# In an attention and MLP kernel, the second weight is split in place, and the planner of the instruction order counts DMA semaphores

## Chip, core and metric

The kernel runs on one core of a Trainium2 chip. The metric is device time in microseconds (us) of one execution. The engines are named as in the profile: PE (TensorE, matmul) with PEld (its weight loads), DVE (VectorE), ACT (ScalarE), POOL (GpSimd) and SP (SyncE, which issues most transfers; ACT issues some too). "SPq" and "ACTq" are the instruction queues of SP and ACT.

## What is computed

Block-sparse attention over 4 batches, 8 heads, 768 positions and head size 64, followed by an MLP of 3072 tokens, 512 to 2048 to 512:

```python
mask = np.abs(blk_i - blk_j) <= window
mask = mask | (blk_i == 0) | (blk_j == 0) | (blk_i == n_blocks - 1) | (blk_j == n_blocks - 1)
for qb in range(n_blocks):
    for kb in sampled_blocks[qb]:
        mask[qb * block:(qb + 1) * block, kb * block:(kb + 1) * block] = True
scores = np.where(mask, scale * np.matmul(q, k.transpose(0, 1, 3, 2)), -1000000000.0)
...
attn = attn / (np.sum(attn, axis=-1, keepdims=True) + 1e-09)
x = np.matmul(attn, v)
...
h = x @ w_in
sp = np.where(h > 20.0, h, np.log1p(np.exp(np.minimum(h, 20.0))))
g = h * np.tanh(sp)
return (g @ w_out).astype(np.float32)
```

Blocks have 32 positions, so there are 24 of them; three sampled blocks belong to each block of queries.

## The kernel before

**Numbers in two halves.** Each large product is made of three float16 products: an operand a is scaled and split into hi (its float16) and lo (the float16 of what is left), and hi x hi, hi x lo and lo x hi are summed in PSUM. The two weights arrive as 64-bit numbers. VectorE decodes them into float32 with three integer instructions per piece (lines 873, 876 and 879). The scale of a weight comes from matmuls of it with itself (`gram`, line 361), a diagonal and a root (`add_gram`, `add_root`, `root`).

**First weight, w_in.** Eight pieces (`piece_i`, `load_i`) are loaded by ACT or SP into a ring of three buffers "wr", decoded and split by TensorE and casts (lines 947 to 956). `scales_w` (line 1016) writes `gsc` when all pieces have their scale.

**Second weight, w_out.** Sixteen chunks of 128x512 (`load_o`, `piece_o`) are loaded into buffers of the ring "raw", which has six and is shared with the loads of q, k and v, and decoded. The float32 of chunk fc takes the whole place `wo[:, fc]`, 2 KiB per partition, in which its hi and lo shall stand. So the split (`parts_o`, which calls `add_split` with `by_pe` false) first writes a scaled copy `wt` into another "raw" buffer (line 963 on ACT or 965 on DVE), casts it to hi (968 or 969), and lets POOL subtract for lo (970).

**Attention.** 52 jobs (13 per batch): a job takes two blocks of queries, or one dense one. It goes through scores (661), maximum (703 to 708), exponential (727), transposes (667), the split of the probabilities (750, 754; in the first three jobs through TensorE, 758 and 763), the product with v (789), division (808 to 811), a transpose and the split of x (836, 839). Its keys are gathered by POOL or ACT (595, 598), its values by SP's transfers from a copy of v in DRAM, "vd" (615 to 622).

**MLP.** Twelve tiles of 256 tokens. `moe_h` (1049) makes the hidden layer of a tile, which takes the x of jobs 0 to 4 for the first one; `moe_g` (1060 to 1099) the activation on ACT, DVE and POOL; `moe_y` (1114) the product with w_out of the tile before, between the pieces of the next tile's hidden layer. The hidden layer's products keep their order, and so do those with w_out. The product of the first half of the first tile with w_out takes all sixteen chunks.

**What sets the order.** `Plan.emit` is a list scheduler: it keeps an estimate of when each engine is free and when each task is ready, and issues, one by one, the task that would start first. Each task has a duration, engines that may run it, the ring buffers that it takes, and a key. The key comes from the call and from three tables, URGE (by kind of tensor), JOBS (by job, the first 14) and PIECES (by piece of a weight). It decides between tasks that could start within 0.02 us of each other; a smaller one goes first. `pace` ranks work on TensorE: the scores of job i are ranked as if they could not start before START[i], but go at once if TensorE has nothing else ready; jobs keep their order. A transfer's end is estimated from its queue alone, by its duration. `fill` puts matmuls without use (line 1309) in front of TensorE's work where it would idle between 14 and 200 us of the plan. On the chip each engine runs its instructions in this order and waits on semaphores. What a task waits for is named by r, what it writes by w.

Of the kernel before, what the change touches and what calls it, by code (L numbers as in the profile page):

```python
# [32 lines left out]
URGE = {"am": -30, "dgi": -29, "endsv": 24, "gh": 8, "gp": -3, "gram": 4, "gramv": 1, "hik": -7, "hiq": 20, "hiv": -7, "hs": 4, "hsw": -16, "k": -4, "kg": -1, "kw": -30, "mx": 19, "nb": -12, "o": 13, "p": -1, "ph": 2, "pl": -30, "q": 12, "r": 30, "rawk": 6, "rawq": 23, "rawv": 24, "s": -10, "sck": 12, "scq": -24, "scv": -3, "ssk": -22, "ssq": 1, "ssv": 9, "t": 14, "tpq": -30, "tpv": 2, "tpw": -12, "tx": -30, "us": -2, "v": -1, "vd": -9, "vg": 1, "wdi": -4, "whi": -3, "who": -30, "wli": -27, "wlo": -11, "wo": 19, "wor": 24, "wq": 7, "wr": -23, "ws": 1, "wto": 26, "xhw": 22, "xw": 10, "ys": -7}  # L33
JOBS = [-17, -8, 5, -19, 0, 1, -8, -9, -24, -11, 1, 1, -4, -26]
PIECES = [-4, -2, -1, 2, -1, 3, 5, 18, -23, -12, -10, -4, -3, -4, 3, 8, 7, 11, 13, 14, 16, 23, 31, 26]
# [29 lines left out]
class Plan:  # L65
# [4 lines left out]
    SEM = 0.06  # L70
# [53 lines left out]
    def emit(self, pace, fill):  # L124
# [6 lines left out]
        free, ready, dma, held = {}, {}, {}, {}  # L131

# [9 lines left out]
        while todo:  # L142
# [66 lines left out]
def attn_mish_kernel(ctx: ExitStack, tc: tile.TileContext, qT, kT, v, sampled, blocks, w_in, w_out, out):  # L209
# [11 lines left out]
    nc = tc.nc  # L221
# [106 lines left out]
    BOTH = True  # L328
# [70 lines left out]
    def add_root(key, ss, fn, r, after, w, new, cls, n=1, apart=False, ring="t"):  # L399

        add("PE", 0.3 * n, lambda: root_pe(key, ss(), apart, ring), r=r, w=[key], new=[(ring, key)], key=cls - 2, lat=0.3)
        add("DVE", 0.6, fn, r=[key, *after], w=w, new=new, key=cls)

    def load(b, what, js, ring="raw", after=()):
# [3 lines left out]
        def fn():  # L408
# [15 lines left out]
            kind=("dma", 1.95 * n))  # L424
# [130 lines left out]
    def globals_v(b, n):  # L555
# [3 lines left out]
        add("SP", 0.9, fn, r=VD3(b), w=[("vg", n)], key=-1, lat=2.3, kind=("dma", 0.5))  # L559
# [46 lines left out]
    def gather_v(su):  # L606
# [6 lines left out]
        def fn():  # L613
# [10 lines left out]
            kind=("dma", 0.9))  # L624

    def fetch_dense(su):
# [11 lines left out]
        for j in T3:  # L638
# [3 lines left out]
                key=-3, lat=2.4, kind=("dma", 2.0))  # L642
# [245 lines left out]
    def load_i(k):  # L888
# [5 lines left out]
        if wide:  # L894
            go = lambda eng: load_w(pools["w"], raw, "wr", src, None, eng)
            add("ACT", 0.45, lambda: go(nc.scalar), r=after, w=[raw], new=[("wr", raw)], key=-9, lat=2.0,
                kind=("dma", 3.9), also=[("SP", 0.5, lambda: go(nc.sync), False)] if BOTH else ())
            return
        add("ACT", 0.45, lambda: load_w(None, None, None, src, a0_i(k).rearrange("p (c f) -> p c f", c=NCC),
                                          nc.scalar), r=after,  # L900
            w=[key], key=-9, lat=2.0, kind=("dma", 1.95))
# [77 lines left out]

    def a0_o(fc):  # L980
        return wo[:, fc].rearrange("p t d -> p (t d)").bitcast(F32)

    def load_o(fc, after=()):
# [3 lines left out]
            key=-5, lat=2.0, kind=("dma", 1.95), also=[("SP", 0.5, lambda: go(nc.sync), False)] if BOTH else ())  # L987
# [47 lines left out]
    def moe_h(st, fp, part):  # L1035
# [17 lines left out]
        for f2 in range(2):  # L1053
            mlp(1.31 if part is None else 0.85, lambda f2=f2: fn(f2), r=[*PARTS_I(fp), *xs], w=[kh, "h in order"],
# [47 lines left out]
    def moe_y(st, m, k, last):  # L1102
# [4 lines left out]
        def fn(h2):  # L1107
# [3 lines left out]
            for f in range(2 * h2, 2 * h2 + 2):  # L1111
                fc = 4 * k + f
                for n, (g, w) in enumerate(((0, 0), (0, 1), (1, 0))):
                    nc.tensor.matmul(tl[ky], tl["g", b, t, k][:, g, f, q], wo[:, fc, w],  # L1114
# [5 lines left out]
        if k == NFC // 4 - 1:  # L1120
# [14 lines left out]
            add("SP", 0.4, out_fn, r=[kys], lat=2.0, kind=("dma", 1.1))  # L1135
# [222 lines left out]
```

## Time and profile before

| What | Value |
|---|---|
| time, median of 3 runs | 788.75 us (786.95 to 789.26) |
| span of the profiled execution, first to last instruction | 786.6 us |
| median less that span | 2.15 us |
| mean granted clock of TensorE | 0.990 |
| HBM read, written | 80.38 MB, 12.95 MB |

The span belongs to one profiled execution, for which no time of its own outside the span is given; the three times are of other executions. So sums made from the profile are made against the span, and the 2.15 us stand between it and the median. In the profile's rows an instruction's line is that of the kernel, "out<-in" are tensors with their buffer numbers left out, and "x16" is a count. A row of waits reads: engine and instruction, what it waited for, us in total, times, the longest.

### The profile page before, as it was taken

The numbers are of one execution on the slowest core, as the hardware profiler recorded it, in microseconds if no ns is written. First come the engines' busy times: TensorE is split into PE (matmuls) and PEld (weight loads), VectorE is DVE, ScalarE is ACT, GpSimd is POOL, SyncE is SP. The second block draws the span as 40 slices with busy tenths as digits, with TensorE's granted clock in tenths as the row PEclk, the third lists the DMA queues.
The fourth block names the chain that finished last, engine by engine and source line by source line (L and its number), as shares of the span: only waits on it lengthen the run. The fifth ranks groups of instructions, "written<-read, shape, count | busy, mean of one in ns | idle before, by whom it ended". The sixth has DMA issues, their size and how long they took to land.

```text
span 786.6 us, 30628 instructions
## 1 busy us (share of the span) xinstructions
PE 740.5 (94%) x12793; PEld 518.7 (66%) x12793; DVE 493.5 (63%) x900; ACT 542.7 (69%) x880; POOL 307.6 (39%) x393
## 2 busy tenths in 40 slices
PE   6677899888999999999999999999999999999997
PEld 5544578665577767767776676677677667666663
DVE  6868988998767764795866457656665453223220
ACT  3555778768868877777887768786876666455650
POOL 2114244887635542374443422534641331213021
PEclk9989999999999999999999999999999999999999
DMA  9878857104534475244346603523444112000000
GB/s 339 263 236 256 268 176 202 44 2 136 159 117 131 119 198 171 69 162 120 87 139 194 192 15 101 174 77 91 119 115 119 37 39 81 14 15 14 14 14 27
DMA packets 57742, 95.31 MB, mean 121 GB/s; under 512 B 8323, under 2 KB 20612, under 8 KB 57604
## 3 DMA queue, kind: packets, MB, share of 16 engines
q1 hardware_dynamic: 52032, 80.51, 34.9%
q10 hardware_dynamic: 5572, 12.85, 4.8%
q8 instruction: 100, 1.64, 0.9%
q14 instruction: 38, 0.31, 0.1%
HBM read 80.38 MB, written 12.95 MB: 119 GB/s over the span
## 4 chain that ended last, share of the span: by engine, by line
PE 73%; DVE 10%; ACT 6%; DMA 5%; issue 2%; POOL 1%; SPq 1%; POOLq 1%; ACTq 0%; DVEq 0%
PE h_None L1049 27%; PE y L1114 26%; PE obank L789 6%; PE t L667 6%; PE s L661 4%; DMA vg<-vd 3%; PE tx L667 1%; PE wd_i L947 1%; DVE wt_o L965 1%; DMA wr<-in_moe_w_in_dram 1%; DVE hs_None L1087 1%; DVE v L491 1%; DMA raw_k<-in_k_dram 1%; ACT us_None L1078 1%; POOL kt L522 1%
## 5 line engine op out<-in xcount | busy, mean ns | idle before, releaser
L1049 PE MATMUL h_None<-xh,wi 128*128 128x256 f16 x1536 | 282.8, 273 | 0.0
L1114 PE MATMUL y<-wo,g 128*128 128x512 f16 x1152 | 278.0, 380 | 4.0 <-POOL wo L970 2.6
L1049 PEld LDWEIGHTS <-wi 128*128 128x128 f16 x2304 | 223.5, 98 | 47.3 <-issue 2.1
L1049 PE MATMUL h_None<-xl,wi 128*128 128x256 f16 x768 | 209.8, 273 | 0.0
L1114 PEld LDWEIGHTS <-g 128*128 128x128 f16 x1152 | 111.1, 98 | 106.7 <-issue 7.3
L1099 POOL TENSOR_TENSOR g<-hs_None,g 128x1024 f16<-128x1024 f32 x48 | 107.6, 2241 | 188.4 <-DVE g L1096 144.8
L598 POOL COPY kg<-kt 128x256 f16 x258 | 107.2, 451 | 123.3 <-PE s L661 109.7
L1060 ACT ACTIVATE hs_None<-h_None,gsc 128x512 f32<-128x512 f32 x96 | 65.5, 684 | 80.2 <-PE h_None L1049 79.4
L727 ACT ACTIVATE pt<-s,nb,ns 128x256 f32<-128x256 f32 (+1 forms) x208 | 106.3, 582 | 5.7 <-PE t L667 5.0
L750 ACT ACTIVATE ph<-t 128x512 f16<-128x512 f32 x112 | 66.5, 596 | 45.1 <-PE t L667 45.0
L754 DVE SCALAR_TENSOR_TENSOR pl<-t,ph 128x512 f16<-128x512 f32 x105 | 71.9, 686 | 35.8 <-ACT ph L750 35.5
L1087 DVE SCALAR_TENSOR_TENSOR hs_None<-us_None,hs_None 128x1024 f32<-128x1024 f32 x48 | 65.0, 1355 | 40.1 <-ACT us_None L1086 40.1
L667 PE MATMUL t<-ident,pt 128*128 128x128 f32 x448 | 70.4, 280 | 6.8 <-DVE pl L754 3.6
L708 DVE TENSOR_REDUCE mx<-s 128x4 f32<-128x1024 f32 x44 | 53.7, 1222 | 31.9 <-PE s L661 31.3
L1083 POOL TENSOR_TENSOR us_None<-us_None 128x1024 f32<-128x1024 f32 x22 | 44.2, 2007 | 71.8 <-DVE us_None L1081 68.7
L667 PEld LDWEIGHTS t<-ident,pt 128*128 128x128 f32 x448 | 51.6, 142 | 21.4 <-DVE pl L754 4.5
L789 PEld LDWEIGHTS <-ph 128*32 128x32 f16 x3584 | 47.9, 94 | 20.9 <-issue 13.1
L1078 ACT ACTIVATE us_None<-hs_None,hsc 128x1024 f32<-128x1024 f32 x48 | 55.2, 1150 | 0.9
L789 PE MATMUL obank<-vg,ph 128*32 128x65 f16 (+1 forms) x3200 | 50.6, 196 | 4.0 <-DMA vg<-vd 2.2
L1081 DVE TENSOR_SCALAR us_None<-us_None 128x1024 f32<-128x1024 f32 x48 | 37.4, 778 | 25.4 <-ACT us_None L1078 25.2
L1085 ACT ACTIVATE us_None<-us_None 128x1024 f32<-128x1024 f32 x48 | 50.7, 1056 | 1.6 <-POOL us_None L1083 0.8
L1086 ACT ACTIVATE us_None<-us_None 128x1024 f32<-128x1024 f32 x48 | 50.7, 1056 | 0.8
(199 smaller groups left out, 893.6 us busy)
## 6 DMA issues: line engine op xcount, KB each, us to landing
vg<-vd SPq DMA_DIRECT2D x320, 65.0 KB, 2.6
vg<-vd SPq DMA_DIRECT2D x80, 195.0 KB, 3.2
wr<-in_moe_w_in_dram ACTq DMA_DIRECT2D x8, 1024.0 KB, 7.4
vd<-v SPq DMA_DIRECT2D x12, 520.0 KB, 3.8
vg<-vd SPq DMA_DIRECT2D x12, 520.0 KB, 5.1
raw_k<-in_k_dram SPq DMA_DIRECT2D x12, 512.0 KB, 5.4
raw_q<-in_q_dram SPq DMA_DIRECT2D x12, 512.0 KB, 4.3
raw_v<-in_v_dram SPq DMA_DIRECT2D x12, 512.0 KB, 5.0
```

The lines of the kernel that those rows point to most:

```text
L598: nc.gpsimd.tensor_copy(out=dst, in_=tl["kt", b][:, :, ds(j, BS)])
L667: nc.tensor.matmul(out, src, ident, start=start, stop=stop, is_transpose=True)
L727: ex = lambda o, x, g, w: nc.scalar.activation(out=o, in_=x, func=AF.Exp, bias=nb[:, g, w:w + 1], scale=tl["ns", b, sus[w]["qb"] // TB][:, ...
L750: nc.scalar.activation(out=new(sb, "ph", ("ph", i, j), [P, 2, 2, P], F16), in_=tl["t", i, j], func=AF.Copy, scale=PSC)
L754: nc.vector.scalar_tensor_tensor(out=new(sb, "pl", ("pl", i, j), [P, 2, 2, P], F16), in0=tl["t", i, j], scalar=PSC, in1=tl["ph", i, j], op ...
L789: nc.tensor.matmul(o[cs, w, g, 0:v1 - v0], p[:, k, g, cs], vt[:, k, 2 * c + g, v0:v1], start=j == 0 and g == 0 and k == 0 and n == 0, stop ...
L1049: nc.tensor.matmul(h[:, f2, 0:n].rearrange("p (s q) -> p s q", q=BS), wi[:, fp, cc // 2, w, cc % 2, fs], x[:, s0:s0 + sn, cc], start=f2 == ...
L1060: nc.scalar.activation(out=tl[kq][:, 2 * (fp % 2):2 * (fp % 2) + 2, 0:n], in_=tl[kh][:, :, 0:n], func=AF.Copy, scale=gsc[:, fp:fp + 1])
L1078: nc.scalar.activation(out=us(), in_=hs(), func=AF.Exp, scale=hsc[:, b:b + 1])
L1087: add("DVE", 1.32 * c, lambda: nc.vector.scalar_tensor_tensor(out=hs(), in0=us(), scalar=-0.5, in1=hs(), op0=ALU.add, op1=ALU.mult), r=[ku ...
L1099: add("POOL", 2.3 * c, lambda: nc.gpsimd.tensor_tensor(out=g(1), in0=hs(), in1=g(0), op=ALU.subtract), r=[kq, ("gh",) + kp], w=[kp], use=[kg])
L1114: nc.tensor.matmul(tl[ky], tl["g", b, t, k][:, g, f, q], wo[:, fc, w], start=fc == 0 and n == 0, stop=fc == NFC - 1 and n == 2)
```

## The change

There are four parts.

1. The second weight is split without the copy and without POOL. Chunk fc is cast from its float32 to hi with the scale in the same instruction (ACT or DVE), and DVE makes lo as float32 x scale - hi with one scalar_tensor_tensor. The halves go to `wo_at(fc)`, the place of the chunk two before, whose float32 is used up by then; the first two go to new room "wx" in the pool of the MLP (4 KiB per partition). So a cast waits for hi and lo of the chunk two before, or, for chunks 0 and 1, for the pool to be open.
2. In `add_root` the matmul waits for what the VectorE half waited for (`after`), and `moe_h` waits for `gsc`.
3. The planner counts eight semaphores ("lanes") for the transfers that SP and ACT issue and eight for POOL's. Transfers take them in turn, whatever their queue, and one starts only when the transfer eight before it has landed. A task names how many transfers it has, and some durations are new.
4. URGE, JOBS, PIECES and START have new values. In URGE most of the 50-odd entries change, by up to some 50 (the two long lines are left out below).

```diff
-JOBS = [-17, -8, 5, -19, 0, 1, -8, -9, -24, -11, 1, 1, -4, -26]
-PIECES = [-4, -2, -1, 2, -1, 3, 5, 18, -23, -12, -10, -4, -3, -4, 3, 8, 7, 11, 13, 14, 16, 23, 31, 26]
+JOBS = [-18, -3, 5, -18, -5, 14, -9, -16, -30, 8, -7, -18, -29, -7]
+PIECES = [-5, -4, -1, -1, 4, 25, 0, 20, -29, -29, 7, -5, -8, -11, 18, 7, 9, -2, 12, 15, 19, 27, 24, 14]
...
-    SEM = 0.06
+    SEM, LANES = 0.06, 8
...
+        lanes = {w: [[0.0] * self.LANES, 0] for w in ("hard", "soft")}
...
+                    if t.kind and t.kind[0] == "dma":
+                        lane, n = lanes["soft" if eng == "POOL" else "hard"]
+                        at = max(at, lane[n % self.LANES])
                     start = self.port(held, eng, max(at, f), t.ways[eng][2])
...
-                other = max([x for e, x in dma.items() if e != t.eng], default=0.0)
-                at = max(dma.get(t.eng, 0.0), end)
-                dma[t.eng] = at + t.kind[1] + min(t.kind[1], 0.5 * max(other - at, 0.0))
-                t.end = max(dma[t.eng], end + t.lat)
+                lane, n, end, t.end = *lanes["soft" if t.eng == "POOL" else "hard"], start, 0.0
+                each = t.kind[1] / t.kind[2]
+                for k in range(n, n + t.kind[2]):
+                    end = max(end, lane[k % self.LANES]) + t.dur / t.kind[2]
+                    other = max([x for e, x in dma.items() if e != t.eng], default=0.0)
+                    at = max(dma.get(t.eng, 0.0), end + 0.3)
+                    dma[t.eng] = at + each + min(each, 0.5 * max(other - at, 0.0))
+                    lane[k % self.LANES] = land = max(dma[t.eng] + 0.5, end + t.lat + min(max(other - end, 0.0), 3.5))
+                    t.end = max(t.end, land)
+                lanes["soft" if t.eng == "POOL" else "hard"][1] += t.kind[2]
+                free[t.eng] = end
...
-        add("PE", 0.3 * n, lambda: root_pe(key, ss(), apart, ring), r=r, w=[key], new=[(ring, key)], key=cls - 2, lat=0.3)
+        add("PE", 0.3 * n, lambda: root_pe(key, ss(), apart, ring), r=[*r, *after], w=[key], new=[(ring, key)], key=cls - 2, lat=0.3)
...
-            kind=("dma", 1.95 * n))
+            kind=("dma", 1.45 * n, n))
...
-            kind=("dma", 0.9))
+            kind=("dma", 1.5, 2 + NR - 1 + (w0 - qb != -1 or w1 - qb != 2)))
...
+    SH = 2
+
+    def wo_at(fc):
+
+        return pools["wx"][:, fc] if fc < SH else wo[:, fc - SH]
...
     def parts_o(fc, cls):
-        if fc == 0:
-            add_diag(("o",), lambda: sc_o, "sc_o", cls)
-        add_split(("o", fc), ("o",), lambda: a0_o(fc), wo[:, fc, 0], wo[:, fc, 1], ("wo", fc), RINGO, cls,
-                  lambda: sc_o, "sc_o", fc % 4 < OPE)
+
+        before = [(w, "o", fc - SH) for w in ("wh", "wl")] if fc >= SH else ["open"]
+        kh, kl = ("wh", "o", fc), ("wl", "o", fc)
+
+        def hi(eng):
+            if eng == "ACT":
+                nc.scalar.activation(out=wo_at(fc)[:, 0], in_=a0_o(fc), func=AF.Copy, scale=sc_o)
+            else:
+                nc.vector.tensor_scalar(out=wo_at(fc)[:, 0], in0=a0_o(fc), scalar1=sc_o, scalar2=None, op0=ALU.mult)
+        add("ACT", 0.62, lambda: hi("ACT"), r=[("wo", fc), "sc_o", *before], w=[kh], key=cls,
+            also=[("DVE", 0.45, lambda: hi("DVE"), True)])
+        add("DVE", 0.72, lambda: nc.vector.scalar_tensor_tensor(
+            out=wo_at(fc)[:, 1], in0=a0_o(fc), scalar=sc_o, in1=wo_at(fc)[:, 0], op0=ALU.mult, op1=ALU.subtract),
+            port=True, r=[("wo", fc), "sc_o", kh], w=[kl], key=cls)
...
-            mlp(1.31 if part is None else 0.85, lambda f2=f2: fn(f2), r=[*PARTS_I(fp), *xs], w=[kh, "h in order"],
+            mlp(1.31 if part is None else 0.85, lambda f2=f2: fn(f2), r=[*PARTS_I(fp), "gsc", *xs], w=[kh, "h in order"],
...
-                    nc.tensor.matmul(tl[ky], tl["g", b, t, k][:, g, f, q], wo[:, fc, w],
+                    nc.tensor.matmul(tl[ky], tl["g", b, t, k][:, g, f, q], wo_at(fc)[:, w],
...
+        pools["wx"] = pools["m"].tile([P, SH, 2, DM], F16, name="wx", tag="wx", bufs=1)
...
-        new=[("hs", ("z",))], key=-9, lat=6.0)
+        new=[("hs", ("z",))], key=-9, lat=6.0, kind=("dma", 0.9, 2 + B))
...
-    RES, START = 595.0, [0, 58, 39, 56, 33, 120, 63, 62, 76, 58, 107, 143, 72, 148]
+    RES, START = 595.0, [4, 107, 38, 81, 33, 149, 115, 59, 5, 106, 122, 170, 16, 77]
```

The other lines give the remaining transfers their count and remove switches that had one value.

More of the change, by code (lines that the diff above doesn't have):

```diff
@@ L28 @@
              wq=2, am=2, dg=2)
-URGE = {"am": -30, "dgi": -29, "endsv": 24, "gh": 8, "gp": -3, "gram": 4, "gramv": 1, "hik": -7, "hiq": 20, "hiv": -7, "hs": 4, "hsw": -16, "k": -4, "kg": -1, "kw": -30, "mx": 19, "nb": -12, "o": 13, "p": -1, "ph": 2, "pl": -30, "q": 12, "r": 30, "rawk": 6, "rawq": 23, "rawv": 24, "s": -10, "sck": 12, "scq": -24, "scv": -3, "ssk": -22, "ssq": 1, "ssv": 9, "t": 14, "tpq": -30, "tpv": 2, "tpw": -12, "tx": -30, "us": -2, "v": -1, "vd": -9, "vg": 1, "wdi": -4, "whi": -3, "who": -30, "wli": -27, "wlo": -11, "wo": 19, "wor": 24, "wq": 7, "wr": -23, "ws": 1, "wto": 26, "xhw": 22, "xw": 10, "ys": -7}
-JOBS = [-17, -8, 5, -19, 0, 1, -8, -9, -24, -11, 1, 1, -4, -26]
-PIECES = [-4, -2, -1, 2, -1, 3, 5, 18, -23, -12, -10, -4, -3, -4, 3, 8, 7, 11, 13, 14, 16, 23, 31, 26]
+URGE = {"am": -10, "dgi": -16, "endsv": 24, "gh": -20, "gp": -30, "gram": 17, "gramk": -27, "gramq": 30, "gramv": 13, "hik": -30, "hiq": 22, "hiv": 24, "hs": -13, "hsw": -18, "k": 25, "kg": 9, "kw": -24, "mx": 16, "nb": -18, "o": -2, "p": 1, "ph": 8, "pl": -17, "q": -7, "r": 23, "rawk": -30, "rawq": 17, "rawv": 22, "s": 4, "sck": 25, "scq": -28, "scv": 14, "ssk": -30, "ssq": -13, "ssv": -16, "t": -3, "tpk": -30, "tpq": 5, "tpv": -15, "tx": -15, "us": -11, "v": 18, "vd": -6, "vg": 26, "wdi": -4, "whi": -10, "who": -11, "wi": -4, "wli": -30, "wlo": -15, "wo": 18, "wor": 24, "wq": 5, "wr": -12, "ws": -30, "wto": 26, "xw": 7, "ys": -30}
+JOBS = [-18, -3, 5, -18, -5, 14, -9, -16, -30, 8, -7, -18, -29, -7]
+PIECES = [-5, -4, -1, -1, 4, 25, 0, 20, -29, -29, 7, -5, -8, -11, 18, 7, 9, -2, 12, 15, 19, 27, 24, 14]
 def place(w):
@@ L541, in store_v @@
             out=vd[b][j * TT:(j + 1) * TT].rearrange("(c p) h d -> p c h d", p=P), in_=tl["v", b, j]),
-            r=[("v", b, j)], w=[("vd", b, j)], key=-4, lat=2.5, kind=("dma", 2.0))
+            r=[("v", b, j)], w=[("vd", b, j)], key=-4, lat=2.5, kind=("dma", 2.0, 1))
     KT3 = lambda b: [("k", b, j) for j in T3]
@@ L558, in fn @@
                 nc.sync.dma_start(out=vgs[n][s * BS:(s + 1) * BS, 1], in_=vd[b][j * BS:(j + 1) * BS])
-        add("SP", 0.9, fn, r=VD3(b), w=[("vg", n)], key=-1, lat=2.3, kind=("dma", 0.5))
+        add("SP", 0.9, fn, r=VD3(b), w=[("vg", n)], key=-1, lat=2.3, kind=("dma", 0.5, 2))
     regs = {}
@@ L641, in fetch_dense @@
                 w=[("vg", j) if j < NVG else ("vt", b)], new=[("raw", ("vt", b))] if j >= NVG else (),
-                key=-3, lat=2.4, kind=("dma", 2.0))
+                key=-3, lat=2.4, kind=("dma", 2.0, 1))
     PROD = ((0, 0), (1, 0), (0, 1))
@@ L896, in load_i @@
             add("ACT", 0.45, lambda: go(nc.scalar), r=after, w=[raw], new=[("wr", raw)], key=-9, lat=2.0,
-                kind=("dma", 3.9), also=[("SP", 0.5, lambda: go(nc.sync), False)] if BOTH else ())
+                kind=("dma", 3.9, 1), also=[("SP", 0.5, lambda: go(nc.sync), False)])
             return
         add("ACT", 0.45, lambda: load_w(None, None, None, src, a0_i(k).rearrange("p (c f) -> p c f", c=NCC),
-                                          nc.scalar), r=after,
-            w=[key], key=-9, lat=2.0, kind=("dma", 1.95))
+                                        nc.scalar), r=after,
+            w=[key], key=-9, lat=2.0, kind=("dma", 1.95, 1))
     def piece_i(k, cls):
@@ L986, in load_o @@
         add("ACT", 0.45, lambda: go(nc.scalar), r=after, w=[raw] + ([] if wide else [("wo", fc)]), new=[("raw", raw)],
-            key=-5, lat=2.0, kind=("dma", 1.95), also=[("SP", 0.5, lambda: go(nc.sync), False)] if BOTH else ())
+            key=-5, lat=2.0, kind=("dma", 1.95, 1), also=[("SP", 0.5, lambda: go(nc.sync), False)])
     def piece_o(fc, cls):
@@ L1134, in moe_y @@
                 also=[("ACT", 0.7, lambda: ys_fn("ACT"), False)])
-            add("SP", 0.4, out_fn, r=[kys], lat=2.0, kind=("dma", 1.1))
+            add("SP", 0.4, out_fn, r=[kys], lat=2.0, kind=("dma", 1.1, 1))
     DL = 10
```

3 lines of the change are left out of this document (removed).

## The prediction, made before the changed kernel ran

> **What bounds the kernel now.** I read first the page's busy times and its forty slices, then the stretches between the kernel's stages.
>
> ```profile
> PE 740.5 (94%) x12793; PEld 518.7 (66%) x12793; DVE 493.5 (63%) x900; ACT 542.7 (69%) x880; POOL 307.6 (39%) x393
> PE   6677899888999999999999999999999999999997
> ```
>
> TensorE is busy for 94% of the span, and its low digits stand almost all at the front. The view of stretches (length, then busy time and instructions of each engine, granted clock, DMA share, GB/s) is cut at the first matmul of the hidden layer, at the start and the end of the second weight's split, and at 220 and 700 us:
>
> ```profile
> 0.00:102.60 102.60, 76.87 (x1619) 52.63 (x1619) 80.35 (x181) 59.10 (x116) 25.99 (x54) 0.95 0.84 272
> 102.60:138.00 35.40, 34.16 (x930) 29.49 (x923) 29.23 (x60) 29.31 (x54) 16.87 (x24) 1.00 0.65 183
> 138.00:185.00 47.00, 39.24 (x454) 28.05 (x452) 45.73 (x60) 35.41 (x51) 36.88 (x29) 0.96 0.12 38
> 185.00:220.00 35.00, 33.50 (x634) 19.71 (x633) 27.70 (x45) 26.29 (x43) 24.00 (x27) 1.00 0.45 137
> 220.00:700.00 480.00, 474.93 (x8657) 338.75 (x8656) 291.82 (x537) 352.58 (x577) 186.23 (x253) 1.00 0.39 110
> 700.00:786.60 86.60, 81.79 (x515) 50.09 (x513) 18.70 (x22) 39.98 (x43) 17.66 (x8) 0.99 0.05 19
> L1309 PE MATMUL obank<-neg 128*128 128x240 f16 x109 | 15.6, 282 | 3.8 <-DVE xs L811 3.8
> ```
>
> TensorE's idle time is length less busy: 25.7, 1.2, 7.8, 1.5, 5.1 and 4.8 us, 46.1 in all. The last row is the filler of line 1309, 15.6 us of work without use. So 61 us of the span are not useful TensorE work. From 220 us on there is little to win: 5.1 us in 480, and a tail whose end is the last output. What can move lies before 185 us, in two places.
>
> The first is 138 to 185 us: there VectorE is busy 45.7 of 47 us and TensorE waits. The next fence holds rows of the waits (engine and line, for whom, total us, times, longest), then that window's groups (busy us, mean ns).
>
> ```profile
> PE y L1114 <- POOL wo L970: 2.6, 3, 0.9
> PE t L667 <- DVE pl L754: 3.6, 1, 3.6
> SPq L419 <- POOL wo L970: 22.9, 3, 20.3
> ...
> L965 DVE TENSOR_SCALAR wt_o<-wo,cols 128x512 f32<-128x512 f32 x13 | 11.6, 907 | 0.0
> L1087 DVE SCALAR_TENSOR_TENSOR hs_None<-us_None,hs_None 128x1024 f32<-128x1024 f32 x4 | 9.7, 2416 | 0.0
> L969 DVE CAST wo<-wt_o 128x512 f16<-128x512 f32 x12 | 6.6, 565 | 0.4 <-ACT wt_o L963 0.4
> L1081 DVE TENSOR_SCALAR us_None<-us_None 128x1024 f32<-128x1024 f32 x4 | 6.5, 1618 | 0.1
> L970 POOL TENSOR_TENSOR wo<-wt_o,wo 128x512 f16<-128x512 f32 x16 | 22.6, 1421 | 7.7 <-DVE wo L969 6.4 <-DVE tp_k L394 1.0 <-ACT wo L968 0.3
> ```
>
> The split itself takes 11.6 + 6.6 = 18.2 us of VectorE and 22.6 of the 36.9 us that GpSimd is busy. The two MLP steps beside it, L1087 and L1081, take 2416 and 1618 ns there. Over the whole run their durations (min/median/max) are:
>
> ```profile
> L1087 DVE SCALAR_TENSOR_TENSOR hs_None<-us_None,hs_None x48: 1207/1225/3144, 127.0 to 765.7; 128x1024 f32<-128x1024 f32 x48
> L1081 DVE TENSOR_SCALAR us_None<-us_None x48: 675/693/2627, 116.3 to 761.6; 128x1024 f32<-128x1024 f32 x48
> L965 DVE TENSOR_SCALAR wt_o<-wo,cols x13: 470/639/2353, 138.6 to 177.9; 128x512 f32<-128x512 f32 x13
> L969 DVE CAST wo<-wt_o x12: 411/416/1258, 139.6 to 181.1; 128x512 f16<-128x512 f32 x12
> L876 DVE SCALAR_TENSOR_TENSOR wo<-wor,wo x16: 678/685/885, 66.4 to 126.4; 128x512 int32<-128x512 int32 x16
> L963 ACT ACTIVATE wt_o<-wo,cols x3: 709/712/722, 154.8 to 180.3; 128x512 f32<-128x512 f32 x3
> ```
>
> So VectorE instructions are stretched while GpSimd works. Over the medians that is 4 x (2.416 - 1.225) = 4.8 us for L1087 and 4 x (1.618 - 0.693) = 3.7 us for L1081.
>
> The second place is in front of the first hidden layer matmul, on the chain that ended last (start, length):
>
> ```profile
> 42.59 5.99 DMA vg<-vd
> 48.68 0.38 ACTq L865
> 49.10 0.61 ACT wi L951
> 49.75 0.58 PE wd_i L956
> ```
>
> The waits of that place, and VectorE's decode in order of time, read:
>
> ```profile
> ACT wi L951 <- DMA vg<-vd: 6.4, 1, 6.4
> PE wd_i L956 <- ACT wi L951: 5.5, 1, 5.5
> ...
> 38.83 2.71 DVE L879 SCALAR_TENSOR_TENSOR wi<-wr,wi 128x1024 int32<-128x1024 int32 x2
> ```
>
> ScalarE stands for 6.4 us with a load of w_in at its head. That load goes out at 48.68, 0.1 us after a gather that SyncE started at 42.59 has landed. Its buffer is no reason: the decode that frees one ended at 41.5. So a transfer of one queue held an issue on another, and TensorE lost 5.5 us behind it. The planner of before, which knows no semaphores, could not see this.
>
> **The change, part by part.** *The split (A).* Gone: sixteen scaled copies (13 on VectorE, 3 on ScalarE), sixteen GpSimd subtractions, the one diagonal, and the raw buffers that held the copies. Left: sixteen casts from the float32 (VectorE 0.47 us, the minimum of L965, or ScalarE 0.71, L963). Added: sixteen scalar_tensor_tensor of 128x512 on VectorE, 0.685 us by L876, 11.0 us together. With half the casts on each engine VectorE carries 11.0 + 8 x 0.47 = 14.8 us where it had 18.2, less 3.4. ScalarE carries 8 x 0.71 = 5.7, busy only 35.4 of 47. GpSimd loses 22.6 of 36.9 us, 61%, and I let the stretch of L1087 and L1081 fall by that share: 0.61 x 8.5 = 5.2 us. VectorE's relief is 8.6 us in a stretch where TensorE idles 7.8, so TensorE becomes the bound there. Nothing (something else holds) and 9.3 us (that idle and the 1.5 behind it) are the ends. I take 6.5, nearer the top, because VectorE is the engine without slack in that row.
>
> The new wait, a cast behind both parts of the chunk two before, makes two chains of eight links; a link is 0.71 + 0.685 = 1.4 us, a chain 11.2 us plus handoffs, while the split now spreads over 47. Behind a waiting cast in ScalarE's order stand the exponentials of the MLP, which have 11.6 idle us there. Chunks 0 and 1 need the pool that opens after w_in's decode, long before 138: nothing. The raw buffers no longer wait for GpSimd: the load of v (L419) that stood 20.3 us on SyncE goes out earlier, with the DMA share at 0.12; behind it wait only later loads and gathers. I count that within A.
>
> *Eight semaphores (B).* This adds no instruction; it reorders issues on the SP and ScalarE queues. If the stall at 42.7 goes, 5.5 us of TensorE idle go, if the stages behind follow. But VectorE is busy 80.4 of the 102.6 us, and next late is this:
>
> ```profile
> 92.17 2.08 DVE gsc L1016
> 100.21 0.49 DVE L839 TENSOR_TENSOR xl<-tx,xh 128x128 f16<-128x128 f32 x2
> 102.66 1.42 PE h_None L1049 x12
> ```
>
> The first hidden layer matmul comes 2 us behind the columns of job 4 (L839). The new wait of it for gsc, done at 94.3, costs nothing now and caps what B can bring at 8.4 us. Ends 0 and 8.4; I take 3, about half the stall, as half the rows after it are VectorE's.
>
> *Roots and keys.* The PE half of a root now waits for what its VectorE half waited for anyway: nothing, and it frees a PSUM buffer for other work meanwhile; uncovered, each us by which gsc came after the last needed column would be a us of TensorE. Loads of q, k and v count as 1.45 instead of 1.95 us in the planner, which is order only. The pool of the MLP holds 4 KiB per partition more and nothing waits for that. The keys move everything a little; after 220 us the most they can win is 5.1 us, and by the same row I let them lose as much; I take 0.
>
> Sum: 6.5 + 3 = 9.5 us off the profiled span, 786.6 to 777.1. The median of the runs is 788.75, 2.15 above that span; carried over, the forecast is 779.2.
>
> **The rivals.** *The new subtraction is stretched in its turn.* It reads two tensors from SBUF, as L1087 does, and L1087 took 2416 instead of 1225 ns beside GpSimd, whose other 14.3 us in the stretch stay. Were all sixteen stretched in that ratio, 16 x 0.685 x 0.97 = 10.6 us would eat the relief of 8.6. VectorE stays the bound, A brings nothing, and 788.75 - 3 = 785.8 is left. Against it: L876 of this form, beside GpSimd in part, never took more than 885 ns. [...]
>
> *The semaphores aren't the cause,* or the new order meets others: A alone, 782.2.
>
> *The hidden layer starts later.* START of job 1 goes from 58 to 107, and jobs keep their order, so jobs 2 to 4 follow, whose columns release the first hidden layer matmul. These rows are the scores of jobs 1, 5 and 6:
>
> ```profile
> 35.69 0.24 PE L661 MATMUL s<-kt,q 64*32 64x96 f16 x8
> 90.95 0.24 PE L661 MATMUL s<-kt,q 64*32 64x96 f16 x8
> 98.59 0.24 PE L661 MATMUL s<-kt,q 64*32 64x96 f16 x8
> ```
>
> Jobs follow at 7.6 us. Two such steps put the first hidden layer matmul at 118, cost 15.2 us, and with A, without B, give 788.75 + 15.2 - 6.5 = 797.5. It decides from a start later than 109.1, where it eats A. Against it: START 58 didn't hold job 1, which ran at 35.7, since the value only ranks it against other TensorE work that is ready.
>
> **How the numbers follow.** Forecast 0.46, semaphores no cause 0.20, subtraction stretched 0.20, late start 0.14. A difference under 0.3% (2.4 us) can't be told from none, so the bounds are 786.4 and 791.1. The first two are faster; the stretched case lies at the bound, half of it each way: faster 0.46 + 0.20 + 0.10 = 0.76, within 0.3% 0.10, slower 0.14. The range: A and B at their best give 788.75 - 9.3 - 8.4 = 771, and the keys may add a little, so 770; upward it takes in no gain at all with the keys slightly worse, 790. Left out are the late start and the outer part of the keys, under 0.2.
>
> **What would show it.** Right: no GpSimd work on wo; L1087 and L1081 near their medians in the stretch of the split; TensorE idle there under 2 us; the load of v no longer held by the split; no ScalarE wait of several us for a gather; the first hidden layer matmul before 100. Wrong: VectorE still full and L1087 still near 2.4 us (stretched); a new wait of similar length for a DMA in the first 100 us (semaphores); the first hidden layer matmul after 109 (late start); idle after 220 us well over 5.1 (keys).

## The result and the profile after

| | before | after |
|---|---|---|
| median of 9 runs each, us | 788.84 (786.29 to 792.73) | 795.82 (792.54 to 804.1) |
| ratio, 95% interval | | 1.0107 (1.0073 to 1.0141) |
| span of the profiled execution, us | 786.6 | 792.5 |
| mean granted clock of TensorE | 0.990 | 0.989 |
| first hidden layer matmul, us | 102.7 | 104.6 |

Single executions more than 1.5% above the fastest of their kernel (one of e1, two of e10, two of e13) are left out of the medians and ranges below. The changed kernel is about 7 us, or 1.1%, slower. The forecast was 779.2 us, and its range ended at 790. The page of after shows the busy times and TensorE's forty slices:

```profile
PE 739.9 (93%) x12786; PEld 520.4 (66%) x12786; DVE 492.6 (62%) x897; ACT 546.2 (69%) x882; POOL 288.0 (36%) x377
PE   5787797999999999999899999999999999999997
```

TensorE is busy as long as before (740.5 us), so the longer span is idle time. The view of stretches of after, at the bounds used for before (the last one ends with the span), says where:

```profile
0.00:102.60 102.60, 74.12 (x1499) 50.55 (x1500) 79.47 (x179) 57.41 (x113) 23.82 (x48) 0.95 0.84 263
102.60:138.00 35.40, 31.38 (x933) 26.69 (x931) 29.71 (x53) 26.52 (x54) 21.18 (x28) 0.95 0.63 184
138.00:185.00 47.00, 43.94 (x593) 31.49 (x592) 40.98 (x64) 37.96 (x55) 19.48 (x14) 1.00 0.23 74
185.00:220.00 35.00, 33.57 (x590) 22.24 (x575) 23.16 (x40) 26.79 (x41) 19.67 (x23) 1.00 0.43 130
220.00:700.00 480.00, 468.44 (x8645) 335.03 (x8644) 295.74 (x538) 357.64 (x581) 186.81 (x258) 1.00 0.38 109
700.00:792.50 92.50, 88.46 (x559) 54.38 (x556) 23.57 (x26) 39.87 (x43) 17.05 (x8) 0.99 0.05 18
```

Length less busy gives 28.5, 4.0, 3.1, 1.4, 11.6 and 4.0 us, 52.6 in all, against 46.1 before. The stretch of the split went from 7.8 to 3.1. The first 138 us went from 26.9 to 32.5, and the 480 us of the steady part from 5.1 to 11.6: these two are the loss. (The bounds are times, not stages: in after the same stage can lie elsewhere.)

The split itself came out as meant. The groups of after between 138 and 168 us, where it now runs (busy us, mean ns), and the durations of the new subtraction over the whole run (min/median/max):

```profile
L1032 DVE SCALAR_TENSOR_TENSOR wo<-wo,cols 128x512 f16<-128x512 f32 x14 | 15.3, 1124 | 0.2
...
L1113 DVE SCALAR_TENSOR_TENSOR hs_None<-us_None,hs_None 128x1024 f32<-128x1024 f32 x3 | 3.6, 1215 | 0.0
...
L1107 DVE TENSOR_SCALAR us_None<-us_None 128x1024 f32<-128x1024 f32 x2 | 1.4, 685 | 0.0
```

```profile
L1032 DVE SCALAR_TENSOR_TENSOR wo<-wo,cols x14: 740/750/2626, 141.6 to 166.0; 128x512 f16<-128x512 f32 x14
L1032 DVE SCALAR_TENSOR_TENSOR wx<-wo,cols,wx x2: 751/752/753, 139.2 to 140.4; 128x512 f16<-128x512 f32 x2
```

L1113 and L1107 are the old L1087 and L1081. They are back at 1215 and 685 ns, where they took 2416 and 1618. The stretch passed in part to the new subtraction: 1124 ns in the mean of fourteen, up to 2626, for a median of 750. The four that took 1.4 to 2.6 us each ran beside 0.9 to 2.1 us of GpSimd work; the nine of all sixteen with no GpSimd work beside them took 740 to 753 ns.

Next are the two waits that the semaphores were to remove: a wait of ScalarE, then transfers of the chain from there to the first hidden layer matmul (start, length).

```profile
ACT wi L961 <- DMA vg<-vd: 2.3, 1, 2.3
```

```profile
46.51 8.20 DMA wor<-in_moe_w_out_dram
...
55.98 4.20 DMA vg<-vd
...
60.26 0.33 ACTq L875
...
60.64 0.61 ACT wi L961
...
67.67 9.72 DMA wor<-in_moe_w_out_dram
...
77.91 6.86 DMA wor<-in_moe_w_out_dram
...
93.44 6.49 DMA vg<-vd
```

ScalarE still holds a load of w_in until a gather of SyncE has landed (55.98 + 4.20 = 60.18). The wait is 2.3 us where it was 6.4, but in front of it the chain now has a load of w_out of 8.2 us and behind it two more (9.7 and 6.9 us) and a gather of v of 6.5 us. The first hidden layer matmul starts 1.9 us later than before.

What grew most among the waits of TensorE has no engine or transfer as its releaser. These are the rows "issue", of after and then of before:

```profile
PE s L671 <- issue: 9.4, 3, 4.0
...
PE obank L799 <- issue: 5.2, 6, 1.4
PE obank L1334 <- issue: 2.9, 1, 2.9
...
PE h_None L1075 <- issue: 0.7, 2, 0.4
```

```profile
PE obank L789 <- issue: 5.2, 4, 2.9
...
PE s L661 <- issue: 1.5, 3, 0.9
```

They sum to 18.2 us after and 6.7 before: 11.5 more, in a span that is 5.9 longer. By their place, they went from 4.4 to 9.0 us in the first 138 us and from 2.2 to 8.3 in the steady part, which is most of what these two stretches lost. TensorE's other idle time fell from 39.4 to 34.4 us. The longest stands in TensorE's timeline at 121.8 us, inside one run of scores, whose operands had been there for the matmuls in front of it. The transfers of 118 to 126 us follow.

```profile
121.53 0.26 PE L671 MATMUL s<-kg,q 64*32 64x160 f16 x3
125.81 0.25 PE L671 MATMUL s<-kg,q 64*32 64x160 f16 x4 [4.02 <-issue]
```

```profile
q1 hardware_dynamic: 1753, 1.88, 73.9%
q8 instruction: 1, 0.02, 1.0%
```

Besides 1.88 MB of data there is one transfer of queue 8, whose kind is "instruction". On the page of after that queue has 100 transfers with 1.64 MB, 16 KB each. TensorE has 2 x 12786 instructions (a weight load and a matmul each): 1.64 MB over 25572 is 64 bytes for one, so 16 KB are 256 of them, and 25572 / 256 = 99.9. So queue 8 brings TensorE its own instructions, in blocks of 256. The packed trace has this transfer from 122.95 to 124.28 us, within the stall: 1.2 us before it, 1.3 for it, 1.5 behind it.

The places of the stalls bear this out. If TensorE's instructions are numbered in the order of the packed trace, its semaphore instructions among them, a stall for the end of a block must always come at the same number within 256. It does: in the 20 kernels of this document 173 waits "issue" are longer than 0.4 us, and every one begins after 256 x n + 193 instructions. In front of 171 of them at least 200 of the last 300 matmuls and weight loads were short ones, of scores or of the product with v, and these 300 had run in 2 to 9 us.

### The profile page after: what moved, and what is told of

It reads as the page before. It is cut to its first block, busy times and chain, and to the rows that moved or that the text cites. A ratio compares the mean times of both kernels' runs of the same rounds, so it can differ in the third digit from the quotient of the medians.

```text
span 792.5 us, 30580 instructions
## 1 busy us (share of the span) xinstructions
PE 739.9 (93%) x12786; PEld 520.4 (66%) x12786; DVE 492.6 (62%) x897; ACT 546.2 (69%) x882; POOL 288.0 (36%) x377
## 3 DMA queue, kind: packets, MB, share of 16 engines
q8 instruction: 100, 1.64, 0.9%
## 4 chain that ended last, share of the span: by engine, by line
PE 77%; DVE 8%; DMA 7%; issue 3%; ACT 3%; SPq 1%; POOL 1%; ACTq 0%; DVEq 0%; POOLq 0%
PE y L1140 29%; PE h_None L1075 28%; PE obank L799 6%; PE t L677 6%; PE s L671 4%; DMA wor<-in_moe_w_out_dram 3%; DMA vg<-vd 2%; DVE wo L1032 2%; PE tx L677 1%; PE wd_i L957 1%; DVE wi L889 1%; DMA raw_k<-in_k_dram 1%; DMA raw_v<-in_v_dram 1%; SPq L632 1%; DVE wi L886 1%
## 5 line engine op out<-in xcount | busy, mean ns | idle before, releaser
L1140 PE MATMUL y<-wo,g 128*128 128x512 f16 x1008 | 243.1, 379 | 0.7 <-POOL g L1125 0.7
L1125 POOL TENSOR_TENSOR g<-hs_None,g 128x1024 f16<-128x1024 f32 x48 | 104.2, 2171 | 239.8 <-DVE g L1122 148.4
L608 POOL COPY kg<-kt 128x256 f16 x258 | 114.2, 477 | 139.0 <-PE s L671 127.0
L1113 DVE SCALAR_TENSOR_TENSOR hs_None<-us_None,hs_None 128x1024 f32<-128x1024 f32 x48 | 61.5, 1280 | 39.5 <-ACT us_None L1112 39.5
L1107 DVE TENSOR_SCALAR us_None<-us_None 128x1024 f32<-128x1024 f32 x48 | 36.1, 753 | 57.4 <-ACT us_None L1104 57.2
```

The source lines that it names most:

```text
L608: nc.gpsimd.tensor_copy(out=dst, in_=tl["kt", b][:, :, ds(j, BS)])
L1113: add("DVE", 1.32 * c, lambda: nc.vector.scalar_tensor_tensor(out=hs(), in0=us(), scalar=-0.5, in1=hs(), op0=ALU.add, op1=ALU.mult), r=[ku ...
L1125: add("POOL", 2.3 * c, lambda: nc.gpsimd.tensor_tensor(out=g(1), in0=hs(), in1=g(0), op=ALU.subtract), r=[kq, ("gh",) + kp], w=[kp], use=[kg])
L1140: nc.tensor.matmul(tl[ky], tl["g", b, t, k][:, g, f, q], wo_at(fc)[:, w], start=fc == 0 and n == 0, stop=fc == NFC - 1 and n == 2)
```

## Experiments

The expectations number their theories. Theory 1: the new order, that is the new tables, costs the time. Theory 2: the split itself does. Theory 3: TensorE's waits for its own instructions do; in its later form the places at which blocks of instructions end move the time, whatever the order is good for. Theory 4: the planner that counts does. Theory 5, added after four runs: the tables fit one planner and one set of tasks, and nothing else.

**The split alone (e1)**: the kernel before with the split of the diff (`parts_o`, `wo_at`, the pool "wx") and nothing else.

```diff
-        add_split(("o", fc), ("o",), lambda: a0_o(fc), wo[:, fc, 0], wo[:, fc, 1], ("wo", fc), RINGO, cls,
-                  lambda: sc_o, "sc_o", fc % 4 < OPE)
+        add("ACT", 0.62, lambda: hi("ACT"), r=[("wo", fc), "sc_o", *before], w=[kh], key=cls,
+            also=[("DVE", 0.45, lambda: hi("DVE"), True)])
```

> The split in place alone, in the kernel before: its planner and its four tables stay. If the split is good and the order of the changed kernel is what costs (theory 1), TensorE's idle time from 138 to 185 us falls from 7.8 us to under 4, and the time is 782 to 785. If the split itself costs, by its chains of two or by its VectorE subtraction (theory 2), the time is 790 or more. If waits of TensorE for its own instructions decide (theory 3: before 6.7 us of idle put down to issue, after the change 18.2), the time follows that sum: any order without more of them than before stays below 788.

Measured: 782.13 us (778.02 to 784.97), ratio 0.9918 (0.9891 to 0.9946). The stretch of the split in its profile:

```profile
138.00:185.00 47.00, 47.00 (x698) 34.43 (x696) 41.59 (x67) 43.45 (x68) 30.29 (x23) 1.00 0.24 73
```

TensorE has no idle time left in the 47 us of the split, where it had 7.8. The split is worth 6.7 us, so theory 2 fell and the rest of the change costs 13.7.

**The new tables alone (e2)**: the kernel before with URGE, JOBS, PIECES and START of after.

```diff
-JOBS = [-17, -8, 5, -19, 0, 1, -8, -9, -24, -11, 1, 1, -4, -26]
+JOBS = [-18, -3, 5, -18, -5, 14, -9, -16, -30, 8, -7, -18, -29, -7]
```

> The new URGE, JOBS, PIECES and START alone, in the kernel before, with its split through GpSimd and its planner without semaphores. Theory 1 (the order costs): slower than before, 793 or more. Theory 2 (the split costs): within 3 us of before. Theory 3 (instruction waits): slower only if the idle put down to issue is again well over 6.7 us.

Measured: 806.88 us (803.61 to 812.07), ratio 1.0253 (1.019 to 1.0315). Its waits of TensorE are ordinary ones, and the "issue" rows sum to only 8.1 us:

```profile
PE t L667 <- ACT pt L727: 6.5, 2, 6.1
PE obank L1309 <- DVE xs L811: 6.4, 6, 1.5
...
PE tp_w L385 <- ACT pl L763: 4.5, 1, 4.5
```

With tasks and a planner they do not belong to, the new tables cost 18 us, which theory 3 does not explain. Much of it stands in the plan itself: `fill` puts 25.6 us of matmuls without use (183) into the first 200 us, where before has 15.6 (109).

**All but the new tables (e3)**: after with the four tables of before (the edit of e2 turned round).

> The changed kernel with the four old tables: split in place, roots and gsc, and the planner that counts eight semaphores. Theory 1: 780 to 785, faster than before, and no long stand of ScalarE in front of a load of w_in for a gather. Theory 2: 793 or more. If the counting planner is at fault (theory 4), 793 or more too, but with the split alone fast; then the loads of the weights go out later than before.

Measured: 806.27 us (804.73 to 808.59), ratio 1.0232 (1.0188 to 1.0276). That is 24.1 us behind the split alone, although only the planner, two waits and costs in the planner differ. The new tables are not the culprit by themselves: within the change they win 10.5 us back. The theory of the tables fell, in the form that the old ones would be better in the new kernel.

**All but the counting (e4)**: after with the planner of before, without lanes.

```diff
-                    if t.kind and t.kind[0] == "dma":
-                        lane, n = lanes["soft" if eng == "POOL" else "hard"]
-                        at = max(at, lane[n % self.LANES])
...
+                at = max(dma.get(t.eng, 0.0), end)
+                dma[t.eng] = at + t.kind[1] + min(t.kind[1], 0.5 * max(other - at, 0.0))
+                t.end = max(dma[t.eng], end + t.lat)
```

> The changed kernel whose planner estimates transfers as before, without semaphores; split, roots, gsc and new tables stay. Theory 4 (the counting planner): back to 788 or less. Theory 1 (the tables): 793 or more, as they were set with the counting. Theory 3: whatever the idle put down to issue gives, near 795 at 18 us and near 785 at 7.

Measured: 797.71 us (797.26 to 800.36), ratio 1.0114 (1.0076 to 1.0152). ScalarE's waits for transfers that aren't its own grow again:

```profile
ACT xh L835 <- DMA vg<-vd: 5.8, 1, 5.8
ACT wi L950 <- DMA vg<-vd: 4.4, 1, 4.4
...
ACT wi L950 <- DMA wor<-in_moe_w_out_dram: 3.9, 1, 3.9
```

In after these rows are 2.3 us for a gather and 3.8 for a load of w_out, 6.1 in all against 14.1. The time barely shows it: 1.9 us between e4 and after, at one place of the blocks only. So theory 4, which expected 788 or less, fell. So did theory 3's forecast here, near 785 at 7 us: the "issue" rows of e4 sum to only 5.0 us, at 797.7. Between different orders these waits do not tell the time.

**Old tables, old planner, new waits and load costs (e5)**: the split, `after` in `add_root`, `gsc` in `moe_h`, and three costs in the planner: 1.45 instead of 1.95 us for loads of q, k and v, 1.5 instead of 0.9 for the gathers of v, and 0.9 for the first load of indices, which had none.

```diff
-        add("PE", 0.3 * n, lambda: root_pe(key, ss(), apart, ring), r=r, w=[key], new=[(ring, key)], key=cls - 2, lat=0.3)
+        add("PE", 0.3 * n, lambda: root_pe(key, ss(), apart, ring), r=[*r, *after], w=[key], new=[(ring, key)], key=cls - 2, lat=0.3)
...
-            kind=("dma", 1.95 * n))
+            kind=("dma", 1.45 * n, n))
...
-            kind=("dma", 0.9))
+            kind=("dma", 1.5, 2 + NR - 1 + (w0 - qb != -1 or w1 - qb != 2)))
```

> The changed kernel with the old tables and without the planner's semaphores: the split in place, the roots' and the hidden layer's new waits, and the new load costs. The split alone gave 782.5. If the roots and gsc are as harmless as the prediction has it, 780 to 786. If any new order costs some 15 us against one that the tables were set for (theory 5: the tables fit one planner and one set of tasks, and nothing else), 793 or more, although no table changed.

Measured: 804.07 us (803.22 to 808.19), ratio 1.0199 (1.0162 to 1.0236), where 780 to 786 was expected. This is the part that the prediction held to be free. Its waits of TensorE:

```profile
PE s L660 <- issue: 9.9, 5, 4.4
PE t L666 <- ACT pt L726: 9.2, 2, 6.1
PE obank L788 <- DMA vg<-vd: 8.4, 3, 3.6
...
PE obank L788 <- issue: 4.0, 4, 1.7
```

No row names gsc, and only one, of 0.4 us, the PE half of a root. Two waits and three costs in the planner moved the order, and old tables that had been set for another order met new waits: for probabilities, for gathers, and for instructions (14.5 us in all "issue" rows). Which of the five edits did it was not tried.

e3 is e5 with the planner that counts, and nothing else. ScalarE's waits for gathers are, in e3 and then in e5:

```profile
ACT wi L961 <- DMA vg<-vd: 7.1, 2, 4.5
ACT pl L773 <- DMA vg<-vd: 3.2, 1, 3.2
```

```profile
ACT nb L716 <- DMA vg<-vd: 6.6, 1, 6.6
ACT wi L950 <- DMA vg<-vd: 1.9, 1, 1.9
```

With the old tables, then, the counting shortens nothing (10.3 us against 8.5) and the time is 2.2 us longer. At this one place of the blocks the loss has these steps: from 782.1 (the split) the waits and costs lead to 804.1 (e5), the counting to 806.3 (e3), and the new tables back to 795.8 (after).

**The same order, the blocks moved (e6 to e14, e17, e18).** To part the order from the places of the blocks, 32, 64 or 96 short matmuls into a PSUM bank stand in front of everything. They compute nothing that is needed. Each engine's order stays as it was; only TensorE's blocks end earlier in the work. A matmul is two instructions with its weight load, so 0, 32, 64 and 96 are a block of 256 in quarters, and their mean samples the places of its ends at four points. The matmuls run where TensorE waits for k: in before the first useful one starts at 4.8 us without them, at 6.6 with 64 and 7.9 with 96, but the first root follows at 9.4, 9.0 and 10.0, so little of that delay is left.

```diff
+    for _ in range(64):
+        nc.tensor.matmul(obank[0:32, NO:NO + 65], neg[:, 0, 0:32], neg[:, 1, 0:65], start=True, stop=True)
     plan.emit(pace, fill)
```

On after, 64, 32 and 96:

> The changed kernel with 64 short matmuls without use in front of TensorE's first work, where it waits for k anyway: 128 instructions more, the order otherwise the same. TensorE's instructions come in blocks of 256 (16 KB transfers on queue q8), so the boundaries fall elsewhere. Theory 3 (TensorE waits for its own instructions): the stalls put down to issue move, the one of 4.0 us at 121.8 goes or changes its length, and the time moves by 3 us or more either way. Theory 1 or 5 (the order as such): within 2 us of 795.8, and the same stalls.

> The same with 32 short matmuls, a quarter of a block. Theory 3: another set of stalls and another time, 3 us or more from at least one of the two others. Theory 1 or 5: within 2 us of both.

> The changed kernel with 96 short matmuls in front (795.8, 791.8 and 789.5 with 0, 32 and 64). Theory 3: within that spread, 788 to 797. The mean of the four is what the change costs apart from its boundaries; if it lies at the mean of the shifts of before, boundaries are the whole loss, and if it lies above, the new order costs the rest.

On the split alone, 64, 32 and 96:

> The split alone (782.5 us, 7.7 us of idle beside a fetch of instructions) with the same 64 short matmuls in front. Theory 3: its boundaries were good ones by the choice of its tables, so the idle beside fetches grows and the time with it, 785 or more. Theory 1 or 5: 781 to 784.

> The split alone with 32 short matmuls in front (782.5 without, 792.6 with 64). Theory 3: between 782 and 795, not the same as both; and against the kernel before at the same shift some 6 us faster, as at shift 0, if the gain of the split holds whatever the boundaries.

> The split alone with 96 in front (782.5, 781.0 and 792.6). Theory 3: 780 to 794; if the split's gain is real apart from boundaries, at least 5 us below the kernel before at the same shift.

On before, 64, 32 and 96:

> The kernel before, with 64 short matmuls without use in front, as in the other shifts. Its 788.8 us stand with 10.5 us of idle beside fetches of instructions. If its tables also had good boundaries by selection (theory 3): 793 or more, with 18 us or more of such idle. If the boundaries of before were nothing special: within 3 us of 788.8.

> The kernel before with 32 short matmuls in front. Theory 3: another time than both 788.8 and the shift by 64, by 3 us or more from one of them, mean of the three above 791.

> The kernel before with 96 short matmuls in front (788.8, 796.4 and 803.1 with 0, 32 and 64). Theory 3, with good boundaries by selection at shift 0: 792 to 804, above 788.8. If shift 0 was not special: as likely below.

On e5, 64 and 32:

> The split with the roots' and the hidden layer's new waits and the new load costs, old tables and old planner (804.1 at shift 0, against 782.5 for the split without them), with 64 short matmuls in front. If boundaries make the 21.6 us, this lies under 793, as the other kernels move by 6 to 14. If the order that these small edits lead to is what costs (theory 5), 797 or more here too.

> The same with 32 in front: boundaries, under 793 at one of the two; order (theory 5), 797 or more at both.

Measured, median us and, after the stroke, the sum of TensorE's "issue" waits in the profiled execution:

| matmuls in front | 0 | 32 | 64 | 96 | mean us |
|---|---|---|---|---|---|
| before | 788.8 / 6.7 | 795.6 / 14.8 | 803.1 / 17.8 | 794.6 / 16.7 | 795.5 |
| split alone | 782.1 / 10.8 | 781.0 / 12.2 | 792.6 / 21.9 | 783.0 / 12.5 | 784.7 |
| after | 795.8 / 18.2 | 791.8 / 16.3 | 789.5 / 17.7 | 789.9 / 12.4 | 791.7 |
| e5 | 804.1 / 14.5 | 800.1 / 17.7 | 799.5 / 14.4 | | 801.2 |

Before with 96 in front rests on two executions that lie apart (789.4 and 799.9), too few for a ratio. The unshifted kernel before ran beside each group of runs, with medians from 786.8 to 790.4, so differences of some 3 us between columns say little.

With 64 in front, before takes 1.0176 of its time (1.013 to 1.0222), the split alone 1.0056 of before's (1.002 to 1.0092), and after 1.0013 (0.9986 to 1.004). 64 matmuls without use slow the kernel before by 14 us and speed up the kernel after by 6. The waits of TensorE in before with 64 in front:

```profile
PE s L661 <- issue: 11.4, 5, 5.0
...
PE obank L789 <- issue: 3.4, 2, 2.6
```

The longest of them, 4.98 us, and the clock behind it stand in its stretches from 90 to 110 us; the same stretches of before without the matmuls follow.

```profile
90.00:100.00 10.00, 4.55 (x176) 3.56 (x174) 6.89 (x23) 3.84 (x6) 3.21 (x5) 0.94 1.01 302
100.00:110.00 10.00, 9.99 (x128) 5.40 (x127) 6.90 (x14) 5.93 (x14) 2.33 (x6) 0.72 0.39 123
```

```profile
90.00:100.00 10.00, 8.03 (x263) 5.01 (x252) 9.75 (x23) 7.60 (x16) 4.71 (x8) 1.00 0.93 273
100.00:110.00 10.00, 9.99 (x263) 8.05 (x262) 8.94 (x17) 8.09 (x19) 4.90 (x10) 1.00 0.49 156
```

TensorE idles 5.45 us of ten instead of 1.97, and in the next ten it is as busy, at a clock of 0.72 instead of 1.00, which leaves 7.2 us' worth of full speed. (The counts, 128 and 263, are of different matmuls.) This stall is paid twice. The split alone with 64 in front has a long one too, and a mean clock of 0.88 in its first 102.6 us, where without them it has 0.93:

```profile
PE s L661 <- issue: 10.5, 5, 4.0
...
PE obank L789 <- issue: 4.9, 4, 2.7
```

In before and in the split alone the time follows these waits over the four places. In after the medians hardly do, but each profile is of one execution. The times of the profiled ones are 794.3, 791.8, 796.5 and 785.5 us for waits of 18.2, 16.3, 17.7 and 12.4, and these nearly do. (With 64 in front the profiled one was the slowest of ten, with 96 the fastest.) In e5 they don't: 808.2, 802.0 and 799.0 for 14.5, 17.7 and 14.4, so other waits share the bound there. e5 stayed above 797 at both other places, so by the expectations for e17 and e18 its loss is the order's (theory 5), not that of the places. One expectation was missed: the split with 32 in front was to differ from both its neighbours, but is like the unshifted one.

What follows: at its own place the kernel before stands 6.7 us better than its mean, after 4.1 worse. Compared place by place, after less before is +7.0, -3.8, -13.7 and -4.7 us (mean -3.8); the split alone less before is -6.7, -14.6, -10.5 and -11.6 (mean -10.9); after less the split alone is +13.7, +10.8, -3.1 and +6.9 (mean +7.1). That blocks move the time of one order by up to 14 us is shown, and so is the gain of the split, at all four places. The other two means rest on four places that scatter by more than the mean: the first changes its sign, the second is positive in three of four.

**Short matmuls spaced (e15 on after, e16 on the split alone).** `pace` ranks scores and products with v 1.5 us later once 0.5 us of them has run and not been offset by as much MLP work, once the MLP has begun.

```diff
+                if kind in ("S", "O"):
+                    at["short"] += t.dur
+                elif kind == "M":
+                    at["short"] = max(at["short"] - t.dur, 0.0)
...
+        if kind in ("S", "O") and at["short"] > 0.5 and at["done"] > 0.0:
+            late = max(late, 1.5)
```

> The changed kernel with one rule more in the planner: once the MLP runs, scores and products with v wait for an MLP step when more than 0.5 us of them stand without one between. Theory 3, in its form that the stalls come from blocks of 256 short instructions run through faster than the next is fetched: idle beside fetches after the first hidden layer matmul falls from 10.4 to under 4 us, whatever the boundaries. The time falls by that, if the rest of the order is as good, to about 789. If adjacency isn't the condition: as much such idle as before.

> The split alone with the same rule. It has 4.5 us of idle beside fetches after the first hidden layer matmul. Theory 3: under 2.5 us of it, and 778 to 786, by how well the old tables fit the spaced order. If the tables fit only their own order (theory 5): 790 or more, with the loss outside the fetches.

Measured: 794.27 us (790.63 to 798.05), ratio 1.0113 (1.0074 to 1.0151), and 797.78 us (795.99 to 799.32), ratio 1.0141 (1.0109 to 1.0173). The "issue" waits of e15, then its stretch of the split:

```profile
PE obank L799 <- issue: 2.7, 3, 1.2
...
PE s L671 <- issue: 0.9, 2, 0.7
...
PE obank L1340 <- issue: 0.6, 1, 0.6
```

```profile
138.00:185.00 47.00, 41.42 (x509) 28.42 (x515) 35.17 (x56) 33.87 (x54) 18.80 (x13) 0.93 0.24 77
```

The waits for instructions fell from 18.2 to 4.2 us, as they should if they come from short matmuls that stand together. The time did not fall clearly, by 1.5 us in the medians and not at all in the ratios (1.0113 here, 1.0107 in after); about 789 was expected. TensorE's other idle time rose from 34.4 to 38.9 us: between 138 and 185 us TensorE idles 5.6 us instead of 3.1, at a clock of 0.93 instead of 1.00. In e16 they fell too, from 10.8 to 3.8, but waits like these came instead:

```profile
PE t L667 <- DVE xl L839: 7.1, 1, 7.1
...
PE tx L667 <- ACT pt L727: 4.4, 1, 4.4
```

TensorE's idle time outside the "issue" rows rose from 23.9 us in e1 to 45.1, more than was gained, and the kernel lost 15.7, as theory 5 had it (790 or more, with the loss outside the fetches). So spacing by this rule isn't the cure: it pays with dependencies what it saves on instructions.

The fastest version is the split alone, with the old planner and tables: 782.13 us, and 780.96 (777.23 to 782.57), ratio 0.9901 (0.9866 to 0.9935), with 32 matmuls in front. Both beat before and after; between the two no difference can be told.

## Why the prediction was wrong

**The split (A): right.** It was put at 6.5 us and measured 6.7 by itself; the interval of its ratio gives 4.3 to 8.6, within the ends 0 and 9.3. Its signs held but for one half: idle of TensorE in the stretch was to be under 2 us, and is 0 for e1 but 3.1 in after. L1087 and L1081 are back at their medians, and the load of v is no longer held by GpSimd. Over four places of the blocks the split is worth 10.9, as before had, at its own place, fewer waits for instructions than the split had at any.

**The subtraction stretched in its turn: it did, but too little to decide.** The mean of fourteen was 1124 ns, 64% over the 685 that was forecast, and the rival's price was set at a stretch of 97%. GpSimd's work in 138 to 185 us fell from 36.9 to 19.5 us, and TensorE, no longer VectorE, was the bound in e1 (busy 47.0 of the 47 us, VectorE 41.6).

**Eight semaphores (B): put at 3 us, measured near nothing.** The ScalarE stall fell from 6.4 to 2.3 us. With the new tables the counting shortens such stalls (6.1 us against 14.1), with the old ones it does not (10.3 against 8.5), and the time changes by 1.9 us one way and 2.2 the other. That the semaphores caused the stall in before is therefore not shown. The first hidden layer matmul went from 102.7 to 104.6 us instead of below 100: what came next was not only VectorE's, as the forecast let it be, but also three long loads of w_out and a gather on the chain.

**"Roots and keys": the step that failed.** It said that the PE half of a root waits for what is there anyway, that the load costs are "order only", and that the keys "move everything a little"; its ends were plus and minus 5.1 us, the idle time after 220 us, and 0 was taken. Two things were wrong in it.

- *A bound on what can be won is no bound on what can be lost.* With the tables and the planner left as they were, the waits and costs cost 21.9 us over the split alone (e5 less e1; 16.0 by the means of the three places that both have). The new tables by themselves cost 18 (e2). So the values fit one planner and one set of tasks, as theory 5 has it; in after the tables repair 10.5 of the 24.1 us that the rest spoils.
- *Order also sets where blocks of instructions end.* The prediction had no term for the "issue" rows: they were 6.7 us of before's 46.1 idle, and are 18.2 in after. The kernel before stood at the best of the four places tried, and that its profile was taken there was luck that the prediction could not see.

By the means of the four places the change would gain 3.8 us, and the places of the blocks take 6.7 + 4.1 = 10.8 us back, which leaves the loss of 7.0. That these add up is arithmetic, not a test, and such a division of the loss is no better than four places are.

**The hidden layer starts later: not the cause.** It starts at 104.6, before the 109.1 from which that rival decides. That its price, 797.5, comes near the measured 795.8 is chance. **The sign for the keys held:** "idle after 220 us well over 5.1"; it is 11.6 + 4.0 after, against 5.1 + 4.8 before.

**A sum.** 46.1 + 15.6 is 61.7 us, not 61; nothing hangs on it.

**What stays open.** How the 7.1 us between the split alone and after divide among the counting, the tables and the waits is known at one place of the blocks only (782.1, 804.1, 806.3, 795.8): e3 and e4 have no second one. Which of the two waits and three costs moves the order so far was not tried. Nor was it tried to take the waits for instructions away by fewer, larger matmuls of scores. Why the time of e5 does not follow its waits for instructions isn't known.

## What to carry to other kernels

A set of ranks tuned for a list scheduler belongs to its planner, its task list and its cost values together: change any of them and the time may grow by 2 to 3% (here 18.0 and 21.9 us), so judge the change after the ranks have been set anew. Before trusting a difference of 1% in a kernel with thousands of short matmuls, put 32 or 64 matmuls without use in front of both versions and compare again (here 64 moved the time by 4.6 to 14.3 us); the mean over such places says more than one place. Take the part that the profile proves (here the split, 6.7 us at its own place) and leave the order alone.

## What the runs showed of the hardware

- TensorE waited for its own instructions, 6.7 us in before and 18.2 in after. They came in blocks of 16 KB, 256 instructions, on queue 8, in before and after in 100 transfers of 0.9 to 1.9 us, each begun only shortly before it was needed: in after, transfer n began when between n - 0.4 and n + 0.75 blocks had run, and the sixteenth in the middle of a stall, at 16.75. All 173 waits "issue" over 0.4 us in 20 kernels began at the same place within a block. They lasted 0.4 to 5.0 us in the first 138 us, where the DMA share is 0.63 to 0.84 in before and after, and 0.4 to 3.3 later (medians 1.6 and 1.0).
- 64 matmuls without use at the start moved the time by +14.3 us, +10.5, -6.4 and -4.6 in four kernels.
- A stall of 4.98 us in before with 64 in front was followed by ten us at a mean clock of 0.72, and one of 4.02 in after by six at 0.72; the one of 2.93 us in before left the next 5 us at 1.00. But one of 2.46 us, in before with 64 in front, ended at 37.8 us and was followed by 5 us at 0.50: fifteen matmuls of line 1309 at 41.1 us took 3.16 us, where in before they took 1.70.
